# Converting all weights inside the first batch: other instructions, another place, and keys loaded first

## The chip, the cores and the metric

The kernel runs on one core of one Trainium2 chip, as one program that is launched once. The metric is the device time of an execution in microseconds (us). Engines go by the names that the profile gives them: PE (TensorE matmul), PEld (its weight loads), DVE (VectorE), ACT (ScalarE), POOL (GpSimd), SP (SyncE, which issues all transfers here).

## The reference

```python
def _attn_ref(q, k, v):                      # q, k, v: (8, 8, 576, 64) float32
    scores = scale * np.matmul(q, k.transpose(0, 1, 3, 2))
    kth = np.partition(scores, -top_k, axis=-1)[..., -top_k:-top_k + 1]      # top_k = 32
    scores = np.where(scores >= kth, scores, -1000000000.0)
    attn = np.exp(scores - np.max(scores, axis=-1, keepdims=True))
    attn = attn / (np.sum(attn, axis=-1, keepdims=True) + 1e-09)
    return np.matmul(attn, v)

def _moe_ref(x, w_theta, w_tok_r, w_tok_i, w_ch):     # x: (8, 576, 512), heads side by side
    theta = x @ w_theta
    zr, zi = x * np.cos(theta), x * np.sin(theta)
    y = np.einsum('ts,bsd->btd', w_tok_r, zr) + np.einsum('ts,bsd->btd', w_tok_i, zi)
    u = x + y
    return u + np.maximum(u @ w_ch, 0.0)
```

`reference` runs the attention and gives its output to the mixer `_moe_ref`. The four weight matrices (512x512, 576x576, 576x576, 512x512) arrive as 64-bit floats; the kernel sees each number as two 32-bit integers, a low and a high word, and makes 32-bit floats of them on the chip.

## The kernel before, in words

**Units.** The attention of a batch is done for pairs of heads, four pairs a batch. A pair's 576 queries are five units: four of 128 queries for both heads, and one (`j == NJ`) that holds the last 64 queries of both. So a batch has 20 units, and the kernel has 160. `pipeline` (line 613) walks over them. For unit `i` it emits the search for the 32nd largest score on DVE (`threshold`, `pick`, `fold`: lines 258 to 297, some 25 DVE instructions), the scores of unit `i + 2` (`scores`, line 226: matmuls into `ps_score`, then ACT's copy at line 243), the penalty and the exponential of unit `i - 1` (lines 299 to 315, ACT and POOL), transposes and the product with `v` of unit `i - 2` (lines 317 to 363), and one step of whatever stands in the list `running` (`advance`, line 638).

**Mixer.** When the last unit of a batch is through, `mixer` joins `running`. It turns the attention output, multiplies by `w_theta` (`pth`, lines 467 to 477), takes sine and cosine into the tile `z` (tag "z", a buffer of its own), multiplies by both `w_tok` (`py`, line 576) and by `w_ch` (`po`, line 601). Its matmuls run beside the units of the next batch. Behind the last unit the last mixer runs alone.

**Weights.** `widen_steps` (line 110) is the first entry of `running`: 18 jobs, four for `w_theta` (512 columns), ten for the two `w_tok` (576 columns, the remaining 64 rows of each a job of 64 partitions), four for `w_ch` (512). A job fetches 128 rows (line 129) into a buffer with tag "e", the tag of the score tiles, and converts them: ACT makes integers of the low word (line 139); DVE shifts and masks the high word (140), joins the sign bit to it (141); ACT takes its absolute value (144); POOL adds both (145); DVE sets to zero what was too small (146); for `w_theta` ACT multiplies by a constant (150). Three jobs (`WEARLY`) run ahead of the first unit, 12 steps (`WSTART`) are then let pass, and one job per unit follows. They end inside the second batch, beside the first mixer.

**The first pair.** `split_pair` (line 174) splits queries and keys into a high part (rounded, `kh`, and half of the tile `q2`) and the rest (`kl`, the other half). For the first pair SP loads all of `qT`, then all of `kT`; ACT rounds whole tiles (line 185), DVE subtracts (186).

**What sets the order.** The code gives the instructions in the order above with priorities; the tile framework's scheduler then writes one fixed order per engine, and each engine keeps to it. PSUM has three pairs of buffers: "s" for scores, "t" for transposes, "m" for `px`, `pth`, `py` and `po`.

Of the kernel before, what the change touches and what calls it, by code (L numbers as in the profile page):

```python
# [9 lines left out]
F32 = mybir.dt.float32  # L10
F32R = mybir.dt.float32r
BF16 = mybir.dt.bfloat16
I32 = mybir.dt.int32
U32 = mybir.dt.uint32
AF = mybir.ActivationFunctionType
ALU = mybir.AluOpType
AX = mybir.AxisListType

P = 128
EBUFS = 9  # L20
NQP = 1
WSTART = 12
WEARLY = 3
AHEAD = 2
S_LATE = 0
PLAN = (2, 2, 2, 2, 2)
# [8 lines left out]
STEEP = float(2.0**60)  # L35
LOWEST = -3.0e38
MAGIC = 12582912.0
SMALLEST = 1.125 * 2.0**-15
TWO_PI = 6.283185005187988
INV_TWO_PI = 0.15915494309189535  # L40
HALF_PI = 1.5707963267948966
# [3 lines left out]
def topk_attention_phase_mixer(  # L45
# [11 lines left out]
    nc = tc.nc  # L57
    B, NPAIR, _, S = qT.shape
    DM = w_ch.shape[0]
    D = P // 2  # L60
    H = 2 * NPAIR
    HS = S // 2
    NJ = S // P
    REM = S - NJ * P
    NB = DM // P
    KB = 2 * NJ + 1
# [7 lines left out]
    wk2 = ctx.enter_context(tc.tile_pool(name="wk2", bufs=2))  # L74
    wk3 = ctx.enter_context(tc.tile_pool(name="wk3", bufs=3))
    one = ctx.enter_context(tc.tile_pool(name="one", bufs=1))
    ps_s = ctx.enter_context(tc.tile_pool(name="ps_s", bufs=2, space=bass.MemoryType.PSUM))
    ps_t = ctx.enter_context(tc.tile_pool(name="ps_t", bufs=2, space=bass.MemoryType.PSUM))
    ps_m = ctx.enter_context(tc.tile_pool(name="ps_m", bufs=2, space=bass.MemoryType.PSUM))
# [22 lines left out]

    wts = {}

    def weight_tile(dtype):
        return wk2.tile([P, S], dtype, tag="w", name="w", bufs=2 * NB + KB + 1)

    def widen_steps():  # L110
        for key, n, width in (("ch", NB, DM), ("th", NB, DM), ("tok", KB, S)):
            wts[key] = [weight_tile(F32)[:, :width] for _ in range(n)]
        jobs = []
        for c in range(NB):
            jobs.append((wts["th"][c], w_theta[c * P : c * P + P], slice(0, P), INV_TWO_PI))
        for i, w in enumerate((w_tok_r, w_tok_i)):
            for c in range(NJ):
                jobs.append((wts["tok"][i * NJ + c], w[c * P : c * P + P], slice(0, P), None))
            rows = slice(i * D, i * D + D)
            jobs.append((wts["tok"][2 * NJ][rows], w[NJ * P :], rows, None))  # L120
        for c in range(NB):
            jobs.append((wts["ch"][c], w_ch[c * P : c * P + P], slice(0, P), None))
        held = {}

        def fetch(i):
            dst, src, rows, _ = jobs[i]
            n = dst.shape[-1]
            raw = wk2.tile([P, S, 2], I32, tag="e", name="wraw", bufs=EBUFS)
            nc.sync.dma_start(raw[rows, :n], src.bitcast(I32).rearrange("p (n t) -> p n t", t=2))
            held[i] = raw  # L130

        def convert(i):
            dst, _, rows, factor = jobs[i]
            n = dst.shape[-1]
            raw = held.pop(i)
            tmp = wk2.tile([P, 2, S], I32, tag="e", name="wtmp", bufs=EBUFS)
            word, tail = raw[rows, :n, 1], raw[rows, :n, 0]
            bits, low = tmp[rows, 0, :n], tmp[rows, 1, :n]
            nc.scalar.activation(low, tail.bitcast(U32), AF.Copy, scale=2.0**-29)
            nc.vector.tensor_scalar(bits, word, 3, 0x3FFFFFF8, op0=ALU.logical_shift_left, op1=ALU.bitwise_and)  # L140
            nc.vector.scalar_tensor_tensor(
                bits, word, -0x40000000, bits, op0=ALU.bitwise_and, op1=ALU.bitwise_or
            )
            nc.scalar.activation(word.bitcast(F32), word.bitcast(F32), AF.Abs)
            nc.gpsimd.tensor_add(low, low, bits)
            nc.vector.scalar_tensor_tensor(
                dst, word.bitcast(F32), SMALLEST, low.bitcast(F32), op0=ALU.is_ge, op1=ALU.mult
            )
            if factor is not None:
                nc.scalar.mul(dst, dst, factor)  # L150

        fetch(0)
        for i in range(len(jobs)):
            if i + 1 < len(jobs):
                fetch(i + 1)
            convert(i)
            yield
            if i + 1 == WEARLY:
                for _ in range(WSTART):
                    yield  # L160

    def later(n):
        return tc.high_priority(offset=-n)
# [10 lines left out]
    def split_pair(bq, p, raw):  # L174
        q2 = wk2.tile([P, 2, S], F32R, tag="q2", name="q2")
        kh = wk2.tile([P, 2, S], F32R, tag="kh", name="kh")
        kl = wk2.tile([P, 2, S], F32R, tag="kl", name="kl")
        if raw is None:

            twice = [wk2.tile([P, 2, S], F32, tag="e", name="twice", bufs=EBUFS) for _ in range(2)]  # L180
            for t, src in zip(twice, (qT, kT)):
                for a in range(2):
                    nc.sync.dma_start(t[a * D : a * D + D], src[bq, p].rearrange("(a d) s -> d a s", a=2))
            for t, hi, lo, rows in ((twice[0], q2, q2, slice(D, P)), (twice[1], kh, kl, slice(0, P))):
                nc.scalar.copy(hi, t)
                nc.vector.tensor_sub(lo[rows], t[rows], hi[rows].bitcast(F32))
        else:
            hi = wk2.tile([P, 2, S], F32R, tag="e", name="hi", bufs=EBUFS)
            nc.scalar.copy(hi, raw)
            nc.gpsimd.tensor_sub(raw.bitcast(F32R), raw, hi.bitcast(F32))  # L190
            st = {n: (hi[:, i].bitcast(F32), raw[:, i]) for i, n in enumerate("qk")}
            for a in range(2):
                sl = slice(a * D, a * D + D)
                for dst, rows, src in (
                    (q2, slice(0, D), st["q"][0]),
                    (kh, slice(0, D), st["k"][0]),
                    (kh, slice(D, P), st["k"][0]),
                    (q2, slice(D, P), st["q"][1]),
                    (kl, slice(0, D), st["k"][1]),
                    (kl, slice(D, P), st["k"][1]),  # L200
                ):
                    nc.sync.dma_start(dst[rows, a].bitcast(F32), src[sl])  # L202
        vt = wk2.tile([P, NJ, P], F32, tag="vt", name="vt")
        vr = vrem[p % 2]
        vsrc = v[bq, :, p * P : p * P + P]
        nc.sync.dma_start(vt, vsrc[: NJ * P].rearrange("(c p) d -> p c d", p=P))
        for a in range(2):
            sl = slice(a * D, a * D + D)
            nc.sync.dma_start(vr[sl, sl], vsrc[NJ * P :, sl])
        return dict(p=p, q2=q2, kh=kh, kl=kl, vt=vt, vr=vr)  # L210
# [402 lines left out]
    def pipeline():  # L613
        NU = NJ + 1
        wsteps = widen_steps()
        total = B * NPAIR * NU
        units, pairs, batches, running = {}, {}, {}, [[wsteps, []]]
# [16 lines left out]
        def split(g):  # L634
            if g < B * NPAIR:
                pairs[g] = split_pair(*divmod(g, NPAIR), pairs.get(g))
# [8 lines left out]
                            break  # L645

        split(0)
        for _ in range(WEARLY):
            next(wsteps)
        for i in range(AHEAD):  # L650
            scores(unit(i))
            fold(unit(i))
# [56 lines left out]
    def plain_batch(bq):  # L709
        bt = new_batch(bq)  # L710
        for p in range(NPAIR):
            pair = split_pair(bq, p, load_pair(bq, p))
            prev = None
            for j in range(NJ + 1):
                u = Unit(bq, bt, p, j, pair, 0, True)
                scores(u)
                fold(u)
                for _ in threshold(u):
                    pass
                penalize(u)  # L720
                exponent(u)
                turn(u, prev)
                mix_values(u)
                keep_values(u)
                prev = u
        for _ in mixer(bt):
            pass

    pipeline()

    redo = nc.values_load(flag, min_val=0, max_val=1)
    with tc.If(redo != 0):
        for _ in widen_steps():
            pass
        with tc.For_i(0, B, 1) as bi:
            plain_batch(bi)
# [38 lines left out]
```

## Time and profile before

| | us |
|---|---|
| median of 3 runs | 1308.04 (1305.59 to 1308.83) |
| the profiled execution, its own time | 1313.39 |
| its span, first to last instruction | 1311.5 |
| busy: PE / DVE / ACT / POOL | 1169.6 / 1181.1 / 1011.9 / 650.6 |

The profiled execution is one execution of its own, 5.35 us above the median of the runs, and 1.9 us of its time lie outside the span. A busy time is that of the engine's instructions, and neighbouring instructions of one engine can overlap by some hundredths of a microsecond. The end of a unit's search is marked by DVE's line 293; the last unit of the first batch has it at 166.9 us, that of the second at 323.4, that of the third at 478.0, and so on to 1216 us for the last; the 95 us behind it are the last mixer.

### The profile page before, as it was taken

The page shows a single profiled execution, that of the slowest core. Times are in us where ns is not written, and L with a number is a line of the kernel's source. Part 1 is how long each engine was busy: PE and PEld are TensorE (multiplying, and loading weights), DVE is VectorE, ACT ScalarE, POOL GpSimd, SP SyncE. Part 2 cuts the span into 40 slices and gives each one's busy share as a digit, 9 for nine tenths or more (in the row PEclk, how much of TensorE's full clock was granted, in tenths as well). Part 3 has the DMA queues.
Part 4 walks back from the last instruction along what each step waited for, and adds up shares of the span by engine and source line. Part 5 has one row for each costly group of instructions (what it writes and reads, how often), then busy time and mean ns, then how long its engine had stood idle before and what let it go on. Part 6 is the DMA issues. An engine that isn't in the chain of part 4 may idle for free.

```text
span 1311.5 us, 21746 instructions
## 1 busy us (share of the span) xinstructions
PE 1169.6 (89%) x6293; PEld 859.9 (66%) x6293; DVE 1181.1 (90%) x3993; ACT 1011.9 (77%) x2072; POOL 650.6 (50%) x768
## 2 busy tenths in 40 slices
PE   3666669899989998899999998899999999899998
PEld 3544445678657775577656785577756786567688
DVE  7999999899999999979999999889999999888453
ACT  4878778978788788977879878886888878786660
POOL 2445655744475445643465534553464544653640
PEclk9878769999989999999999999999998999999999
DMA  5234441433323333123323243123423144120001
GB/s 171 58 84 117 141 125 48 108 82 101 100 63 82 82 110 91 41 76 92 109 55 90 79 113 91 36 59 89 136 55 90 37 115 130 27 64 10 37 2 39
DMA packets 70720, 106.04 MB, mean 81 GB/s; under 512 B 13888, under 2 KB 32064, under 8 KB 70592
## 3 DMA queue, kind: packets, MB, share of 16 engines
q1 hardware_dynamic: 70592, 104.57, 29.5%
q8 instruction: 52, 0.85, 0.3%
q14 instruction: 76, 0.62, 0.2%
HBM read 38.40 MB, written 9.44 MB: 36 GB/s over the span
## 4 chain that ended last, share of the span: by engine, by line
PE 38%; DVE 32%; ACT 15%; issue 4%; POOL 4%; SPq 3%; DMA 3%; ACTq 0%; POOLq 0%; DVEq 0%
PE py L576 14%; DVE lst L283 9%; DVE lst L289 8%; PE pth L472 6%; PE px L357 5%; PE ps_score L234 4%; PE pt L329 3%; DVE lst L265 3%; DVE lo L266 3%; DVE lst L270 3%; SPq L202 3%; ACT e L314 3%; ACT pen L302 2%; PE po L601 2%; ACT e L243 2%
## 5 line engine op out<-in xcount | busy, mean ns | idle before, releaser
L304 POOL TENSOR_TENSOR e<-e,pen 128x576 f32<-128x576 f32 x288 | 369.1, 1299 | 208.4 <-ACT pen L302 195.4
L283 DVE MAX8 lst<-lst 128x8 f32<-128x192 f32 (+3 forms) x1152 | 423.9, 407 | 0.8
L289 DVE MATCH_REPLACE8 lst<-lst 128x192 f32<-128x192 f32 (+2 forms) x864 | 329.7, 388 | 0.0
L576 PE MATMUL py<-w,z 128*128 128x288 f32 x1008 | 272.0, 414 | 1.2 <-DMA z<-whole 1.2
L314 ACT ACTIVATE e<-e,lim 128x576 f32<-128x576 f32 x288 | 225.3, 784 | 36.4 <-POOL e L304 35.1
L234 PE MATMUL ps_score<-kh,q 128*128 128x288 f32 x512 | 188.9, 383 | 59.0 <-DVE lo L266 25.3
L302 ACT ACTIVATE pen<-e,lim 128x576 bf16<-128x576 f32 x288 | 210.7, 775 | 39.5 <-POOL lim L294 39.4
L576 PEld LDWEIGHTS py<-w,z 128*128 128x128 f32 x1008 | 185.7, 193 | 54.4 <-issue 7.1
L329 PE MATMUL pt<-ident,e 128*128 128x128 f32 x1152 | 178.6, 288 | 34.8 <-ACT e L314 21.1
L329 PEld LDWEIGHTS pt<-ident,e 128*128 128x128 f32 x1152 | 141.0, 146 | 76.4 <-ACT e L314 27.2
L357 PE MATMUL px<-at,vt 128*64 128x320 f32 (+1 forms) x1024 | 171.0, 430 | 7.7 <-ACT at L334 5.3
L243 ACT COPY e<-ps_score 128x576 f32<-128x576 f32 x256 | 162.0, 647 | 18.9 <-PE ps_score L234 14.7
L331 ACT COPY at<-pt 128x512 f32<-128x512 f32 x256 | 145.2, 587 | 28.0 <-PE pt L329 27.3
L234 PE MATMUL ps_score<-kl,q 128*128 128x288 f32 x512 | 157.5, 323 | 4.5 <-DMA kl<-raw 3.9
L234 PEld LDWEIGHTS ps_score<-kh,q 128*128 128x128 f32 x512 | 104.7, 205 | 81.9 <-ACT e L243 23.1
L265 DVE TENSOR_TENSOR lst<-ps_score,e 128x576 f32<-128x576 f32 (+1 forms) x160 | 109.6, 685 | 46.0 <-ACT e L243 20.9
L357 PEld LDWEIGHTS px<-at,vt 128*64 128x64 f32 x1024 | 78.4, 142 | 70.2 <-issue 19.5
L601 PE MATMUL po<-xt,w 128*128 128x288 f32 x448 | 119.4, 407 | 0.0
L270 DVE MAX8 lst<-lo 128x8 f32<-128x288 f32 x288 | 116.8, 441 | 0.0
L234 PEld LDWEIGHTS ps_score<-kl,q 128*128 128x128 f32 x512 | 105.8, 207 | 11.6 <-DMA kl<-raw 4.2
L472 PE MATMUL pth<-w,xt 128*128 128x512 f32 x224 | 107.4, 626 | 5.0 <-ACT xt L450 5.0
L266 DVE TENSOR_TENSOR lo<-ps_score,e 128x576 f32<-128x576 f32 (+1 forms) x160 | 109.6, 685 | 0.0
(119 smaller groups left out, 1676.5 us busy)
## 6 DMA issues: line engine op xcount, KB each, us to landing
kh<-hi SPq DMA_DIRECT2D x124, 144.0 KB, 2.7
kl<-raw SPq DMA_DIRECT2D x124, 144.0 KB, 2.6
raw<-in_qT_dram SPq DMA_DIRECT2D x31, 288.0 KB, 3.0
raw<-in_kT_dram SPq DMA_DIRECT2D x31, 288.0 KB, 3.1
q<-hi SPq DMA_DIRECT2D x62, 144.0 KB, 2.5
q<-raw SPq DMA_DIRECT2D x62, 144.0 KB, 2.6
vt<-in_v_dram SPq DMA_DIRECT2D x32, 256.0 KB, 2.9
out_dram<-ot SPq DMA_DIRECT2D x28, 288.0 KB, 2.2
```

The costliest lines, as they stand in the source:

```text
L234: nc.tensor.matmul(out[:, at : at + n], l, r, start=(i == 0), stop=(i == len(mm) - 1), skip_group_check=True)
L243: nc.scalar.copy(u.x[:, :, keys], u.ps[:, :, :HS])
L270: nc.vector.max(u.lst[:, w, HS:TOP], u.lo1[:, w])
L283: nc.vector.max(lst[:, w, best], part[w])
L289: nc.vector.match_replace(out=rest, in_to_replace=lst[:, w, best], in_values=part[w], imm_value=LOWEST)
L302: nc.scalar.activation(pen[:, w], u.x[:, w], AF.Relu, bias=u.lim[:, w, 0:1], scale=-STEEP)
L304: nc.gpsimd.tensor_sub(u.x[:, w], u.x[:, w], pen[:, w])
L314: nc.scalar.activation(u.x[:, w], u.x[:, w], AF.Exp, bias=u.lim[:, w, 1:2], scale=SCALE, accum_out=acc)
L329: nc.tensor.transpose(pt[:, c], e[:, w, at0 : at0 + P], ident)
L357: nc.tensor.matmul(px[sl, :n], pr["vt"][:, kb, sl], pr["at"][:, a, kb], start=(kb == 0), stop=False, skip_group_check=True)
L472: nc.tensor.matmul(th[j][: l.shape[-1]], l, r, **pos)
L576: nc.tensor.matmul(py[:, :HS], l, r, start=(i == 0), stop=(i == len(mm) - 1))
```

## The change

All 17 jobs (the two 64-row remainders are one job now) start two steps after the first unit and go on one per unit, so that they end inside the first batch. The raw words and the intermediate values lie in the first mixer's `z` buffer (`room`, two raw buffers and two intermediate ones) in place of "e" buffers. The arithmetic is another: ACT writes the scaled absolute value of the high word into a PSUM tile `size` with tag "m" (in two halves where the job has 576 columns), DVE takes the maximum with a constant there and shifts it into `room`, ACT takes the sign, POOL adds the low word and multiplies by the sign. The first pair is loaded keys first, queries in two pieces, and rounded and subtracted in pieces.

```diff
-WSTART = 12
-WEARLY = 3
+WSTART = 2
@@ widen_steps
-            rows = slice(i * D, i * D + D)
-            jobs.append((wts["tok"][2 * NJ][rows], w[NJ * P :], rows, None))
+        jobs.append((wts["tok"][2 * NJ], [w[NJ * P :] for w in toks], None))
...
+        room = one.tile([P, KB * DM], I32, tag="z", name="room")
+        raws = [room[:, i * 2 * S : (i + 1) * 2 * S].rearrange("p (n t) -> p n t", t=2) for i in range(2)]
+        tmps = [room[:, (i + 2) * 2 * S : (i + 3) * 2 * S].rearrange("p (t n) -> p t n", t=2) for i in range(2)]
...
             nc.scalar.activation(low, tail.bitcast(U32), AF.Copy, scale=2.0**-29)
-            nc.vector.tensor_scalar(bits, word, 3, 0x3FFFFFF8, op0=ALU.logical_shift_left, op1=ALU.bitwise_and)
-            nc.vector.scalar_tensor_tensor(
-                bits, word, -0x40000000, bits, op0=ALU.bitwise_and, op1=ALU.bitwise_or
-            )
-            nc.scalar.activation(word.bitcast(F32), word.bitcast(F32), AF.Abs)
+            m = n if n <= DM else n // 2
+            for c in range(0, n, m):
+                size = ps_m.tile([P, 512], F32, tag="m", name="size")[:, :m]
+                nc.scalar.activation(size, sign[:, c : c + m], AF.Abs, scale=2.0**16)
+                nc.vector.tensor_scalar(size, size, SMALLEST, None, op0=ALU.max)
+                nc.vector.tensor_scalar(bits[:, c : c + m], size.bitcast(I32), 3, None, op0=ALU.logical_shift_left)
+            nc.scalar.activation(sign, sign, AF.Sign)
             nc.gpsimd.tensor_add(low, low, bits)
-            nc.vector.scalar_tensor_tensor(
-                dst, word.bitcast(F32), SMALLEST, low.bitcast(F32), op0=ALU.is_ge, op1=ALU.mult
-            )
+            nc.gpsimd.tensor_mul(dst, low.bitcast(F32), sign)
@@ split_pair, first pair
-            for t, src in zip(twice, (qT, kT)):
+            for t, src, cols in ((tk, kT, slice(0, S)), (tq, qT, q0), (tq, qT, q1)):
...
-            for t, hi, lo, rows in ((twice[0], q2, q2, slice(D, P)), (twice[1], kh, kl, slice(0, P))):
-                nc.scalar.copy(hi, t)
-                nc.vector.tensor_sub(lo[rows], t[rows], hi[rows].bitcast(F32))
+            for w in range(2):
+                nc.scalar.copy(kh[:, w], tk[:, w])
+                nc.vector.tensor_sub(kl[:, w], tk[:, w], kh[:, w].bitcast(F32))
+            for cols in (q0, q1):
+                nc.scalar.copy(q2[:, :, cols], tq[:, :, cols])
+                nc.vector.tensor_sub(q2[D:, :, cols], tq[D:, :, cols], q2[D:, :, cols].bitcast(F32))
@@ pipeline
-        for _ in range(WEARLY):
-            next(wsteps)
```

Here `q0` is the first 128 query columns and `q1` the other 448. The constant of the maximum is 2.25.

How the instructions move, in three places. ACT at the program's start; before, conversions (lines 139 to 150) stand ahead of the first copy of scores (line 243):

```order
L185 CAST q_100<-twice 128x1152
L185 CAST kh<-twice 128x1152
L215 COPY qpad_95<-q_100 128x64 x2
L139 ACTIVATE wtmp<-wraw 128x512
L144 ACTIVATE wraw<-wraw 128x512
L139 ACTIVATE wtmp<-wraw 128x512
L144 ACTIVATE wraw<-wraw 128x512
L150 ACTIVATE w<-w 128x512
L139 ACTIVATE wtmp<-wraw 128x512
L243 COPY e<-ps_score 128x2x288 x2
```

and of the change (its line 252 is line 243 of before, and its 143, 147 and 150 are a job's three steps on ACT):

```order
L191 CAST kh<-twice 128x576 x2
L194 CAST q_100<-twice 128x2x128
L194 CAST q_100<-twice 128x2x448
L252 COPY e<-ps_score 128x2x288
L224 COPY qpad_95<-q_100 128x64 x2
L252 COPY e<-ps_score 128x2x288
L143 ACTIVATE room<-room 128x512
L147 ACTIVATE size<-room 128x512
L252 COPY e<-ps_score 128x2x288
```

The two casts become four, and the first copy of scores now follows them at once. DVE in the second batch, where the first mixer's angles are taken (line 487 before, 496 in the change); before:

```order
L487 SCALAR_TENSOR_TENSOR z<-whole,pth 128x512
L289 MATCH_REPLACE lst<-lst 128x277 x2
L283 MAX lst<-lst 128x8 x2
L146 SCALAR_TENSOR_TENSOR w<-wraw,wtmp 128x512
L283 MAX lst<-lst 128x8 x2
L289 MATCH_REPLACE lst<-lst 128x240 x2
L140 TENSOR_SCALAR wtmp<-wraw 128x512
```

and of the change:

```order
L496 SCALAR_TENSOR_TENSOR z<-whole,pth 128x512
L292 MAX lst<-lst 128x8
L298 MATCH_REPLACE lst<-lst 128x192 x2
L443 TENSOR_TENSOR xs<-px_s,rinv 64x256 x2
L292 MAX lst<-lst 128x8 x2
L302 TENSOR_REDUCE lst<-lst 128x2
L292 MAX lst<-lst 128x8 x2
```

No conversion is left beside the first mixer. ACT in the first batch, some 12 units in; before, one job's two steps (139, 144) among the work of two units:

```order
L139 ACTIVATE wtmp<-wraw 128x512
L314 ACTIVATE e,sums<-e,lim 128x576
L302 ACTIVATE pen<-e,lim 128x576 x2
L144 ACTIVATE wraw<-wraw 128x512
L369 COPY xt<-px 128x320
L331 COPY at_978<-pt 128x4x128
```

and of the change, some eight units in:

```order
L147 ACTIVATE size<-room 128x288
L143 ACTIVATE room<-room 128x576
L323 ACTIVATE e,sums<-e,lim 128x576
L311 ACTIVATE pen<-e,lim 128x576
L340 COPY at_832<-pt 128x4x128
L147 ACTIVATE size<-room 128x288
L252 COPY e<-ps_score 128x2x288
L150 ACTIVATE room<-room 128x576
```

A job has four steps on ACT here where it had two. The number of activation table loads is the same in both orders.

## Rows read from the trace of the kernel before

**Rows 1.** The page, first part: busy time, share of the span, instructions.
```profile
PE 1169.6 (89%) x6293; PEld 859.9 (66%) x6293; DVE 1181.1 (90%) x3993; ACT 1011.9 (77%) x2072; POOL 650.6 (50%) x768
```
**Rows 2.** Stretches, batches 1 to 4 and 6: length; PE, PEld, DVE, ACT, POOL busy; PEclk, DMA.
```profile
17.75:166.90 149.15, 95.38 (x468) 73.36 (x466) 147.86 (x500) 114.09 (x232) 75.94 (x86) 0.81 0.36 97
166.90:323.40 156.50, 139.01 (x707) 99.40 (x708) 151.53 (x493) 126.79 (x256) 88.67 (x98) 0.90 0.34 92
323.40:478.00 154.60, 146.64 (x802) 108.57 (x801) 150.42 (x534) 128.94 (x265) 80.31 (x98) 0.97 0.32 85
478.00:625.00 147.00, 137.93 (x749) 99.75 (x748) 135.23 (x476) 117.28 (x244) 72.30 (x91) 0.99 0.31 81
...
771.50:925.60 154.10, 145.52 (x791) 105.18 (x790) 139.83 (x487) 120.32 (x251) 74.72 (x91) 0.99 0.30 80
```
**Rows 3.** Timeline of the first 18 us: start, length, engine, line, operation, idle before.
```profile
2.19 1.26 SPq L183 DMA_DIRECT2D twice<-in_kT_dram  x2
...
6.31 1.15 ACT L185 CAST q<-twice 128x1152 fp32r<-128x1152 f32 x1 [4.07 <-DMA twice<-in_qT_dram]
...
8.98 1.15 ACT L185 CAST kh<-twice 128x1152 fp32r<-128x1152 f32 x1 [1.52 <-DMA twice<-in_kT_dram]
...
10.18 0.85 PE L234 MATMUL ps_score<-kh,q 128*128 128x288 f32 x2 [10.18 <-ACT kh L185]
...
12.94 0.44 PE L234 MATMUL ps_score<-kl,q 128*128 128x288 f32 x1
...
16.34 1.15 ACT L243 COPY e<-ps_score 128x576 f32<-128x576 f32 x2
...
17.75 0.75 DVE L265 TENSOR_TENSOR lst<-ps_score,e 128x576 f32<-128x576 f32 x1
```
**Rows 4.** DVE busy in the first two batches, lines 140, 141, 146 in turn.
```profile
17.75:166.90 149.15, 3.09 (x7) 0.81 0.36 97
166.90:323.40 156.50, 4.52 (x8) 0.90 0.34 92
17.75:166.90 149.15, 6.18 (x8) 0.81 0.36 97
166.90:323.40 156.50, 8.14 (x8) 0.90 0.34 92
17.75:166.90 149.15, 7.70 (x8) 0.81 0.36 97
166.90:323.40 156.50, 6.90 (x9) 0.90 0.34 92
```
**Rows 5.** DVE groups by form, 0 to 240 us: busy, mean ns.
```profile
L434 DVE TENSOR_TENSOR xs<-px_s,rinv 128x512 f32<-128x512 f32 x4 | 2.7, 675 | 0.0
L266 DVE TENSOR_TENSOR lo<-ps_score,e 128x288 f32<-128x288 f32 x6 | 2.7, 446 | 0.0
```
**Rows 6.** DVE timeline near 151 us, two neighbours.
```profile
150.86 0.44 DVE L265 TENSOR_TENSOR lst<-ps_score,e 128x288 f32<-128x288 f32 x1
151.22 0.44 DVE L266 TENSOR_TENSOR lo<-ps_score,e 128x288 f32<-128x288 f32 x1
```
**Rows 7.** Line 140 alone: ns min/median/max, first and last start us.
```profile
L140 DVE TENSOR_SCALAR wtmp<-wraw x18: 420/440/1492, 11.4 to 231.5; 128x512 int32<-128x512 int32 x8, 128x576 int32<-128x576 int32 x8, 64x576 int32<-64x576 int32 x2
```
**Rows 8.** ACT and POOL groups by form, 0 to 240 us.
```profile
L144 ACT ACTIVATE wraw<-wraw 128x576 f32<-128x576 f32 x8 | 6.0, 746 | 4.1 <-DVE wtmp L141 4.1
L144 ACT ACTIVATE wraw<-wraw 128x512 f32<-128x512 f32 x8 | 5.5, 681 | 2.7 <-DVE wtmp L141 2.7
L334 ACT COPY at<-pt 128x256 f32<-128x256 f32 x10 | 3.2, 378 | 1.7 <-PE pt L329 1.7
L145 POOL TENSOR_TENSOR wtmp<-wtmp 128x576 int32<-128x576 int32 x8 | 11.2, 1410 | 4.8 <-DVE wtmp L141 2.5 <-PE pt L329 2.2
```
**Rows 9.** Stretches of 12 us, columns as in rows 2.
```profile
42.00:54.00 12.00, 8.86 (x52) 6.79 (x52) 12.00 (x47) 11.39 (x25) 5.77 (x9) 0.86 0.17 51
246.00:258.00 12.00, 10.74 (x58) 7.42 (x57) 10.03 (x35) 11.20 (x25) 6.69 (x11) 1.00 0.46 124
```

More of the change, by code (lines that the diff above doesn't have):

```diff
@@ L37 @@
 MAGIC = 12582912.0
-SMALLEST = 1.125 * 2.0**-15
+SMALLEST = 1.125 * 2.0
 TWO_PI = 6.283185005187988
@@ L114, in widen_steps @@
         for c in range(NB):
-            jobs.append((wts["th"][c], w_theta[c * P : c * P + P], slice(0, P), INV_TWO_PI))
-        for i, w in enumerate((w_tok_r, w_tok_i)):
+            jobs.append((wts["th"][c], (w_theta[c * P : c * P + P],), INV_TWO_PI))
+        toks = (w_tok_r, w_tok_i)
+        for i, w in enumerate(toks):
             for c in range(NJ):
-                jobs.append((wts["tok"][i * NJ + c], w[c * P : c * P + P], slice(0, P), None))
-            rows = slice(i * D, i * D + D)
-            jobs.append((wts["tok"][2 * NJ][rows], w[NJ * P :], rows, None))
+                jobs.append((wts["tok"][i * NJ + c], (w[c * P : c * P + P],), None))
@@ L121, in widen_steps @@
+        jobs.append((wts["tok"][2 * NJ], [w[NJ * P :] for w in toks], None))
         for c in range(NB):
-            jobs.append((wts["ch"][c], w_ch[c * P : c * P + P], slice(0, P), None))
-        held = {}
+            jobs.append((wts["ch"][c], (w_ch[c * P : c * P + P],), None))
+        room = one.tile([P, KB * DM], I32, tag="z", name="room")
+        raws = [room[:, i * 2 * S : (i + 1) * 2 * S].rearrange("p (n t) -> p n t", t=2) for i in range(2)]
+        tmps = [room[:, (i + 2) * 2 * S : (i + 3) * 2 * S].rearrange("p (t n) -> p t n", t=2) for i in range(2)]
@@ L125, in fetch @@
         def fetch(i):
-            dst, src, rows, _ = jobs[i]
-            n = dst.shape[-1]
[L128 to L138, printed above, removed]
-            nc.scalar.activation(low, tail.bitcast(U32), AF.Copy, scale=2.0**-29)
-            nc.vector.tensor_scalar(bits, word, 3, 0x3FFFFFF8, op0=ALU.logical_shift_left, op1=ALU.bitwise_and)
-            nc.vector.scalar_tensor_tensor(
-                bits, word, -0x40000000, bits, op0=ALU.bitwise_and, op1=ALU.bitwise_or
-            )
-            nc.scalar.activation(word.bitcast(F32), word.bitcast(F32), AF.Abs)
+            dst, srcs, _ = jobs[i]
@@ new lines, in fetch, with convert @@
+            n = P // len(srcs)
+            for k, src in enumerate(srcs):
+                nc.sync.dma_start(
+                    raws[i % 2][k * n : k * n + n, : dst.shape[-1]],
+                    src.bitcast(I32).rearrange("p (n t) -> p n t", t=2),
+                )
+        def convert(i):
+            dst, _, factor = jobs[i]
+            n = dst.shape[-1]
+            word, tail = raws[i % 2][:, :n, 1], raws[i % 2][:, :n, 0]
+            bits, low = tmps[i % 2][:, 0, :n], tmps[i % 2][:, 1, :n]
+            sign = word.bitcast(F32)
+            nc.scalar.activation(low, tail.bitcast(U32), AF.Copy, scale=2.0**-29)
+            m = n if n <= DM else n // 2
[5 more added lines that the diff above has]
+            nc.scalar.activation(sign, sign, AF.Sign)
@@ L152, in widen_steps @@
         fetch(0)
+        for _ in range(WSTART):
+            yield
         for i in range(len(jobs)):
@@ L157, in widen_steps @@
             yield
-            if i + 1 == WEARLY:
-                for _ in range(WSTART):
-                    yield
     def later(n):
@@ L178, in split_pair @@
         if raw is None:
-            twice = [wk2.tile([P, 2, S], F32, tag="e", name="twice", bufs=EBUFS) for _ in range(2)]
-            for t, src in zip(twice, (qT, kT)):
+            tq, tk = [wk2.tile([P, 2, S], F32, tag="e", name="twice", bufs=EBUFS) for _ in range(2)]
+            q0, q1 = slice(0, P), slice(P, S)
+            for t, src, cols in ((tk, kT, slice(0, S)), (tq, qT, q0), (tq, qT, q1)):
                 for a in range(2):
-                    nc.sync.dma_start(t[a * D : a * D + D], src[bq, p].rearrange("(a d) s -> d a s", a=2))
-            for t, hi, lo, rows in ((twice[0], q2, q2, slice(D, P)), (twice[1], kh, kl, slice(0, P))):
-                nc.scalar.copy(hi, t)
-                nc.vector.tensor_sub(lo[rows], t[rows], hi[rows].bitcast(F32))
+                    nc.sync.dma_start(
+                        t[a * D : a * D + D, :, cols], src[bq, p, :, cols].rearrange("(a d) s -> d a s", a=2)
+                    )
+            for w in range(2):
[4 more added lines that the diff above has]
+                nc.vector.tensor_sub(q2[D:, :, cols], tq[D:, :, cols], q2[D:, :, cols].bitcast(F32))
         else:
```

## The prediction

> **What bounds the kernel now.** I read the page's busy times first. DVE with 90% and PE with 89% share the kernel [rows 1], so the question is which of them ends last where. The stretches by batch answer it [rows 2]. In the first batch, from the first search on, DVE is busy for 147.86 of 149.15 us and PE for only 95.38: no mixer runs yet, and DVE alone sets the pace. In the second batch DVE has 151.53 of 156.50 and PE 139.01. From the third on PE is the fuller engine, with 93.8 to 94.9% in the three later rows shown; DVE is down to 135 to 140 us in the fourth and sixth. So a microsecond taken from DVE is worth a microsecond in the first batch, part of one in the second, and little behind it. The start is a third place: the timeline shows DVE's first search at 17.75 us [rows 3], and everything later hangs on it.
>
> **The start.** Before, `q` is loaded first and rounded at 6.31; `kT` is issued from 2.19, rounded at 8.98; the first scores start at 10.18 and the last of the first unit's are begun at 12.94. Yet ACT copies them only at 16.34, because in its fixed order conversions stand ahead of that copy [rows 3]. With the change keys take the first place in SP's queue, so I let them land where queries did, at 6.3. ACT rounds two halves of about 0.6 (half of 1.15) to 7.5; the first 128 query columns are 2/9 of a tensor that took 2.7 us to follow the other (6.31 to 8.98), so they are there by 7.0; their cast ends near 7.9. DVE subtracts in pieces behind that, to about 8.8. Eight matmuls then need the 2.3 us that the old ones need without their gap, so scores end near 11.1, the first copy has been made meanwhile, and the search starts at 11.3: **minus 6.5 us**. Bounds: minus 7 if a cast hides better, minus 5 if the query piece lands with the whole tensor, at 9.0. Three early conversions lay in this gap on DVE; they cost nothing there before and now have to be paid in the first batch, below. What is queued behind `q`, `vt` and the first weights, is not needed before 11 us.
>
> **DVE in the first batch.** What goes: lines 140, 141 and 146 took 3.09, 6.18 and 7.70 us there, 17.0 in 23 instructions [rows 4]. Neighbours overlap by 0.08: the one at 150.86 is 0.44 long, and the next starts after 0.36 [rows 6]. So 23 x 0.08 = 1.9 goes off: 15.1 us are freed. What comes: all 17 jobs, two passes over PSUM each: 8 jobs of 512 columns are 16 instructions, 9 of 576 are 36 of 288 columns. The trace has no `tensor_scalar` on PSUM. Its DVE reads of PSUM take 675 ns for 512 columns and 446 for 288 [rows 5], that is 0.59 and 0.36 in the queue; in SBUF line 140 takes 420 at the least and 440 in the median, over widths of 512 and 576 [rows 7]. I take the PSUM rows, which share the memory with the new instruction: 16 x 0.59 + 36 x 0.36 = 22.4 us. **Net plus 7.3 us.** By the SBUF row, 0.34 for 512 and an estimated 0.20 for 288, it would be 12.6 us, net minus 2.5. The other bound is that the write to PSUM and the pass behind it, which reads what the first wrote, cost a third more: 30 us, net plus 15.
>
> The rows show two speeds, a median of 440 ns for 512 and 576 columns in SBUF and 446 for 288 in PSUM [rows 5, 7]. The Trainium skill (VectorE: DVE Perf Modes, "Why PSUM operands drop a tier") says that a 32-bit operand in PSUM loses the mode with two read ports that a `tensor_scalar` in SBUF has. By that rule the sum stays at plus 7.3, and without it would be at minus 2.5; no run here shows it for this instruction yet.
>
> **The second batch.** The three lines had 4.52 + 8.14 + 6.90 = 19.6 us there in 25 instructions [rows 4], 17.6 in the queue, and all of it goes. DVE then needs about 134 of the 156.5 us, and PE's 139 set the end. The fourth batch, with 137.93 of PE and 135.23 of DVE, takes 147.0 [rows 2]; I let the second do the same: **minus 9.5 us**. Bounds: minus 2.2, if it takes the 154.3 (mean) of the third and sixth, and minus 17.6, all of DVE's part. From there on the batches hold the same work as before; the orders differ in detail, which I price at plus or minus 4 us.
>
> **ACT in the first batch.** A job has two steps of about 0.71 on ACT before [rows 8], 8 jobs there 11.4 with a multiplication of 0.7. The change has three of 0.68 for 512 columns, and for 576 two of 0.746 and two of 288 columns, estimated 0.40 from the 256-column row [rows 8]: 8 x 2.04 + 9 x 2.29 + four multiplications of 0.68 = 39.6, less 4 for overlaps of neighbours. So ACT goes from 114.09 to some 138 us of 149.15 + 7.3 = 156.5: 88%. Does DVE wait then? At 11.39 of 12 us on ACT, DVE ran on without a gap; at 11.20 of 12, in another stretch, it had 10.03 [rows 9]. I estimate that two thirds of the batch would be that full: the bounds are zero and 105/12 x 2.0 = 17 us. I take the low end, **plus 2 us**, because scores are made two units ahead and ACT has slack in the stretches between.
>
> **POOL, PSUM, SP.** POOL gets 34 instructions of at most 1.41 and loses 8 [rows 8], so 75.94 goes to about 112 us of 156: nothing, while ACT's and DVE's work covers it; without that cover an exponential waits up to 2.8 us for a job in front of its subtraction. `size` shares the pair "m" with `px`: the product with `v` can wait for a shift on DVE, and PE has 54 us of idle time in this batch to hide that. A fetch on SP waits for POOL's multiplication two jobs back, and copies of the next pair stand behind it; they have two units. The buffer "z" is free when the first mixer's angles come, units after the last job.
>
> **Sum**: -6.5 + 7.3 - 9.5 + 2.0 = -6.7 us. The profiled execution took 1313.39, so it would be 1306.7; against the median of the runs, 5.35 lower, **1301.3 us**.
>
> **Rivals.**
> *A. The second batch does not get shorter.* It takes 154.3, as the third and sixth do, the sixth with 139.83 of DVE [rows 2], little more than the 134 that it will have. For it: PE at 95% there, and the order holds the first mixer's last products back until the third batch. Against: the fourth. -6.5 + 7.3 - 2.2 + 2.0 = +0.6: 1308.6.
> *B. ACT becomes the bound of the first batch* (slower). ACT keeps an order too; if its waits for POOL, PE and transfers stay what they are, its idle time of 149.15 - 114.09 = 35 us comes on top of 138: 173 in place of 156.5, plus 16.5 instead of 2: +7.8, 1315.8. It decides from 18.5 us of idle time on, and the kernel is slower from some 30. For it: the full stretch with DVE at 10.03. Against: the idle time is there because DVE sets the pace, so it should shrink.
> *C. DVE's passes in PSUM run at SBUF's pace.* -2.5 in place of +7.3: 1291.5, less if ACT then bounds. Against it: rows 5; for it, nothing but line 140.
> *D. The change doesn't do what it says*: a sign function could bring table loads on ACT. Both orders have equally many, so I leave it 2%.
>
> **How the numbers follow.** Forecast 50%, with its own range 1296 to 1307; A 22%; B 18%; C 8%; D 2%. A measurement of this kernel can tell some 0.3% from no change, here 3.9 us: faster is below 1304.1, slower above 1312.0. The forecast gives 38 points to faster and 12 to no change; C gives 8 to faster; A, with the spread of 4, 7 to faster, 11 to no change, 4 to slower; B 14 to slower, 4 to no change; D 2 to no change: 0.53, 0.29, 0.18. The range must hold A and the middle of B, and leave out C's end: 1293 to 1315.
>
> **What would show it.** In the profile after: the first search at 11 to 12 us; the maximum and the shift with 0.67 us for 512 columns and 0.45 for 288, none stretched; the first batch's end near 167 as before, the second's near 314; ACT at 85 to 90% of the first batch with DVE above 97%. Wrong would be: DVE waiting for ACT's copies or for `size` in the first batch (B), a second batch of 154 us with PE at 95% (A), or half-length passes (C). It would be wrong altogether if later batches, whose work is the same, differed by more than 4 us in sum.

## The result: 1.1% faster, and the profile after

| | before | after |
|---|---|---|
| median of 6 runs, us | 1309.09 (1305.59 to 1313.34) | 1295.1 (1290.59 to 1298.9) |
| ratio to before, 95% interval | | 0.9891 (0.9863 to 0.9919) |
| the profiled execution, us | 1313.39 | 1298.9 |

The change takes 14.0 us off, clear of what the measurement can't tell from no change. The forecast was 1301.3; the time lies in the range, but the gain is twice the 6.7 us of the sum. A second measurement of the unaltered change, in another session, gave 0.9894 (0.9873 to 0.9915).

The stretches of the profile after, first batch to fourth, columns as in [rows 2]; the batches end here by the last search of a batch (line 302 on DVE, line 293 before):

```profile
11.00:167.44 156.44, 103.10 (x469) 73.53 (x467) 155.00 (x529) 134.20 (x277) 101.93 (x109) 0.72 0.44 128
167.44:300.30 132.86, 119.80 (x624) 85.08 (x625) 128.28 (x458) 112.49 (x233) 76.08 (x92) 0.95 0.30 76
300.30:454.50 154.20, 148.10 (x805) 107.35 (x805) 142.54 (x496) 122.29 (x254) 75.06 (x93) 0.99 0.30 79
454.50:598.40 143.90, 137.37 (x740) 99.14 (x737) 136.66 (x481) 119.73 (x248) 76.98 (x93) 0.98 0.32 85
```

The first batch ends at 167.44 us, as before (166.9): it begins earlier and is longer. DVE is busy for 155.00 of its 156.44 us, so ACT, with 134.20, can have cost it 1.4 us at the most. The second batch looks 24 us shorter than the 156.50 of [rows 2], but searches and mixer are shifted against each other in the new order, and the third, with 154.20, is longer than the third before. For that one [rows 2] has a wrong mark, and with it for the fourth and the sixth. The last unit of a batch holds 64 queries of both heads in one list of 128, so its row of line 293 writes 128x1. The row behind 478.0 writes 128x2: it is the first unit of the fourth batch.

```profile
464.52 0.14 DVE L293 TENSOR_REDUCE lst<-lst 128x1 f32<-128x4 f32 x1
477.93 0.15 DVE L293 TENSOR_REDUCE lst<-lst 128x2 f32<-128x8 f32 x1
```

The third, fourth and sixth batches before, at their true ends, columns as in [rows 2]:

```profile
323.40:464.50 141.10, 133.14 (x718) 97.83 (x717) 136.92 (x485) 118.83 (x245) 74.85 (x93) 0.96 0.31 82
464.50:615.60 151.10, 142.03 (x777) 102.64 (x778) 139.33 (x490) 119.68 (x248) 73.91 (x91) 0.99 0.31 81
758.80:916.10 157.30, 148.72 (x808) 107.09 (x808) 142.55 (x496) 120.67 (x252) 72.47 (x90) 0.99 0.29 78
```

A fairer mark than the end of a search is the end of a mixer. DVE's last row of the first and of the second mixer (start, length, line, operation), before:

```profile
338.13 0.44 DVE L602 SCALAR_TENSOR_TENSOR ot<-po,xt 128x288 f32<-128x288 f32 x1
...
492.36 0.43 DVE L602 SCALAR_TENSOR_TENSOR ot<-po,xt 128x288 f32<-128x288 f32 x1
```

and after:

```profile
331.80 0.43 DVE L611 SCALAR_TENSOR_TENSOR ot<-po,xt 128x288 f32<-128x288 f32 x1
...
480.18 0.43 DVE L611 SCALAR_TENSOR_TENSOR ot<-po,xt 128x288 f32<-128x288 f32 x1
```

By these marks the span's 14.4 us come as +0.5 up to the first batch's end (167.44 for 166.9), -12.7 from there to the second mixer's end (480.18 - 167.44 = 312.7 for 325.5), and -2.2 behind it (to 1297.1 and 1311.5).

Of the 12.7 us, 6.9 come up to the first mixer's end (331.80 - 167.44 = 164.4 for 171.2) and 5.8 between both ends (148.4 for 154.2). Where the first part arises is seen in the 36 us behind the first batch. Two stretches of 18 us before, columns as in [rows 2]:

```profile
168.00:186.00 18.00, 12.13 (x53) 7.81 (x53) 18.00 (x52) 12.25 (x26) 12.10 (x10) 0.69 0.42 125
186.00:204.00 18.00, 14.46 (x54) 9.10 (x56) 17.81 (x52) 14.33 (x28) 10.41 (x11) 0.66 0.56 159
```

and after:

```profile
168.00:186.00 18.00, 14.17 (x70) 9.90 (x71) 18.00 (x66) 15.12 (x34) 12.74 (x16) 0.81 0.55 145
186.00:204.00 18.00, 16.79 (x80) 9.74 (x79) 17.52 (x60) 13.84 (x30) 7.18 (x11) 1.00 0.01 5
```

DVE is full in all four, or nearly so. Before, conversions take 2.27 + 5.55 + 2.94 = 10.8 us of its 36 there (lines 140, 141, 146); after, two last ones end within the first eight. PE does 150 matmuls in place of 107, at a granted clock of 0.81 and 1.00 in place of 0.69 and 0.66. The clock matters for what a busy microsecond is worth: from one matmul to the next, scores of 288 columns take 0.24 us where these traces have a granted clock of 0.50 and 0.13 where they have 1.00, transposes 0.21 and 0.11, `py` 0.48 and 0.24. Counted with the steps at 1.00 (0.13 us for scores and, on average, for `px`, 0.11 for a transpose, 0.24 for `py` and `po`, 0.43 for `pth`), PE has done 61 us of work by 168 us in both kernels, and 77 before and 85 after by 204. So PE's 26.6 busy microseconds of these 36 before held only 16 us of work. The lead of 8 us lasts, at 194 and 201 us of work by 336 us, as PE is full from about 250 us to the first mixer's end in both.

The second part arises behind it, where no conversion runs in either kernel. From the first mixer's end to the second's, before and after:

```profile
338.13:492.36 154.23, 145.50 (x790) 107.21 (x786) 150.25 (x533) 127.66 (x266) 78.11 (x97) 0.97 0.33 86
331.80:480.18 148.38, 142.18 (x771) 102.95 (x769) 136.72 (x477) 119.22 (x246) 74.29 (x89) 0.99 0.31 82
```

By the first mixer's end, 41 units' searches were through before and 43 after; by the second's, 62 in both. Before, DVE still catches up two units there and is busy for 150.25 of 154.23 us. That this backlog is what costs the 5.8 us fits the rows; no experiment isolates it.

The start, rows of the timeline as in [rows 3]:

```profile
6.32 1.24 ACT L191 CAST kh<-twice 128x576 fp32r<-128x576 f32 x2 [4.07 <-DMA twice<-in_kT_dram]
...
8.96 0.61 PE L243 MATMUL ps_score<-kh,q 128*128 128x288 f32 x1 [8.96 <-DVE q L195]
...
10.32 0.64 ACT L252 COPY e<-ps_score 128x576 f32<-128x576 f32 x1 [0.72 <-PE ps_score L243]
...
11.28 0.64 ACT L252 COPY e<-ps_score 128x576 f32<-128x576 f32 x1
...
11.96 0.76 DVE L274 TENSOR_TENSOR lst<-ps_score,e 128x576 f32<-128x576 f32 x1 [1.23 <-ACT e L252]
```

The search starts at 11.96 us in place of 17.75. The new DVE passes, groups by form from 0 to 240 us (busy, mean ns, idle before):

```profile
L148 DVE TENSOR_SCALAR size<-size 128x288 f32<-128x288 f32 x18 | 8.1, 456 | 0.0
L149 DVE TENSOR_SCALAR room<-size 128x288 int32<-128x288 int32 x18 | 7.9, 444 | 0.0
L148 DVE TENSOR_SCALAR size<-size 128x512 f32<-128x512 f32 x8 | 5.5, 687 | 0.1
L149 DVE TENSOR_SCALAR room<-size 128x512 int32<-128x512 int32 x8 | 5.4, 675 | 0.0
```

They take what reads of PSUM took before [rows 5], and 26.9 us in all, against 42 for lines 140, 141 and 146. One job, with a pass of each line, still falls behind the first batch's end.

### The profile page after: what moved, and what is told of

Read it like the earlier page. It is cut to its first block, busy times and chain, and to the rows that moved or that the text cites. A ratio compares the mean times of both kernels' runs of the same rounds, so it can differ in the third digit from the quotient of the medians.

```text
span 1297.1 us, 21711 instructions
## 1 busy us (share of the span) xinstructions
PE 1168.7 (90%) x6293; PEld 852.4 (66%) x6293; DVE 1165.8 (90%) x3993; ACT 1018.5 (79%) x2098; POOL 663.1 (51%) x784
## 4 chain that ended last, share of the span: by engine, by line
DVE 32%; PE 32%; ACT 22%; POOL 4%; SPq 3%; issue 3%; DMA 3%; ACTq 0%; DVEq 0%; POOLq 0%
PE py L585 11%; DVE lst L292 10%; DVE lst L298 9%; PE pth L481 6%; PE px L366 4%; ACT e L323 4%; ACT pen L311 4%; DVE lst L274 3%; DVE lo L275 3%; DVE lst L279 3%; ACT e L252 3%; PE ps_score L243 3%; SPq L211 3%; ACT at L340 3%; PE pt L338 2%
## 5 line engine op out<-in xcount | busy, mean ns | idle before, releaser
L313 POOL TENSOR_TENSOR e<-e,pen 128x576 f32<-128x576 f32 x288 | 365.3, 1286 | 195.2 <-ACT pen L311 184.3
L292 DVE MAX8 lst<-lst 128x8 f32<-128x296 f32 (+3 forms) x1152 | 424.1, 406 | 0.9
L298 DVE MATCH_REPLACE8 lst<-lst 128x277 f32<-128x277 f32 (+2 forms) x864 | 329.2, 386 | 0.0
L243 PE MATMUL ps_score<-kh,q 128*128 128x288 f32 x512 | 186.3, 378 | 56.4 <-DVE lo L275 30.9
L366 PE MATMUL px<-at,vt 128*64 128x320 f32 (+1 forms) x1024 | 174.9, 440 | 4.5 <-ACT at L343 4.5
```

The lines of the kernel that those rows point to most:

```text
L243: nc.tensor.matmul(out[:, at : at + n], l, r, start=(i == 0), stop=(i == len(mm) - 1), skip_group_check=True)
L292: nc.vector.max(lst[:, w, best], part[w])
L298: nc.vector.match_replace(out=rest, in_to_replace=lst[:, w, best], in_values=part[w], imm_value=LOWEST)
L313: nc.gpsimd.tensor_sub(u.x[:, w], u.x[:, w], pen[:, w])
L366: nc.tensor.matmul(px[sl, :n], pr["vt"][:, kb, sl], pr["at"][:, a, kb], start=(kb == 0), stop=False, skip_group_check=True)
```

## The experiments

The theory: DVE sets the pace of the first batch, PE that of what follows as soon as DVE doesn't hold it up any more; the change gains because it takes conversions from DVE behind the first batch and makes them cheap enough for the first. Each experiment moves one part. Every run stands against before in its own session. Each edit lets the scheduler write another order of the whole program, so a difference of a few us has two sources; the last experiment measures that.

### Keys first alone

```diff
+ before.py, with the new loading and splitting of the first pair; WEARLY = 3, WSTART = 12 stay
```

> The kernel before with only the new loading of the first pair (keys first, in pieces). Theory (DVE sets the pace of the first batch, and its start is set by ACT's fixed order): three conversions still stand ahead of the first copy of scores, so the first search starts only about 1 us earlier than 17.75, and the time is 1306 to 1310 where before has 1309. Rival (the gain of the change is the earlier loading): the first search near 12 us and 1303 or less.

Measured: 1307.13 us, ratio 1.0001 (0.9982 to 1.0019). The search starts at 17.08. ACT's timeline shows why:

```profile
15.10 0.65 ACT L139 ACTIVATE wtmp<-wraw 128x512 int32<-128x512 uint32 x1
15.66 1.15 ACT L249 COPY e<-ps_score 128x576 f32<-128x576 f32 x2
```

The copies of scores wait behind the third job's first step, as before. The earlier keys alone gain nothing.

### The new place with the old arithmetic

```diff
-WSTART = 12
-WEARLY = 3
+WSTART = 2
+ fetch(0), then WSTART steps let pass, then a job per unit; keys first; lines 139 to 146 and the "e" buffers stay
```

> Keys first and all jobs from the second step on, one per unit, but with the old arithmetic (three DVE instructions a job) and the old buffers. Theory: first search near 12 us, first batch longer than the change's by some 18 jobs x 2.1 us less 26 us of the change = 10 to 15 us, so its last search ends near 180 us; the second batch gains as in the change: 1303 to 1309. Rival (only the place counts, DVE's passes do not): 1295 as in the change.

Measured: 1310.52 us, ratio 1.0015 (0.9997 to 1.0033), a little past the theory's 1309 and far from the rival. The search starts at 11.65, but the first batch ends at 183.07 only, 15.6 us behind the change. One stretch from 12 us to that end, and the old passes by form:

```profile
12.00:183.00 171.00, 106.27 (x471) 79.11 (x470) 170.25 (x537) 130.13 (x255) 94.29 (x96) 0.75 0.41 117
```

```profile
L140 DVE SCALAR_TENSOR_TENSOR wtmp<-wraw,wtmp 128x576 int32<-128x576 int32 x8 | 7.6, 952 | 0.0
...
L139 DVE TENSOR_SCALAR wtmp<-wraw 128x512 int32<-128x512 int32 x8 | 6.6, 819 | 0.0
```

DVE is full (170.25 of 171). Its old passes cost 40 us there, where those of the change cost 26.9. The one in SBUF that takes 420 ns at best [rows 7] has a mean of 819 in the eight passes of 512 columns; the eight of 576 columns have 483. The long mean comes of two passes, of 1185 and 2428 ns, that ran beside an instruction of POOL:

```profile
149.94 2.63 POOL L194 TENSOR_TENSOR raw<-raw,hi 128x1152 fp32r<-128x1152 f32 x1 [0.63 <-ACT hi L193]
150.42 2.43 DVE L139 TENSOR_SCALAR wtmp<-wraw 128x512 int32<-128x512 int32 x1
```

The Trainium skill (SBUF — State Buffer, "Who interferes with whom") says that DVE and GpSimd share a pair of ports as a lock, which such a pass and one with two SBUF inputs need, and an instruction outside the two-port modes with one SBUF input at most does not. The runs agree: of the change's 26 maxima, many beside a busy POOL, none took more than 700 ns.

```profile
L148 DVE TENSOR_SCALAR size<-size x26: 445/460/700, 13.8 to 168.2; 128x288 f32<-128x288 f32 x18, 128x512 f32<-128x512 f32 x8
```

### The new arithmetic in the old place

```diff
+ before.py's place (WEARLY = 3, WSTART = 12) and "e" buffers, keys first
+ line 139, then Abs into size (PSUM), max and shift on DVE, Sign on ACT, add and multiply on POOL
```

> Keys first and the new arithmetic (PSUM, sign by GpSimd), but the old buffers and the old place (three jobs ahead, the others one per unit from the twelfth unit on). Theory: DVE is relieved by some 4 us in the first batch and 6 to 8 in the second, of which PE takes a part: 1300 to 1304. Rival (place counts, arithmetic does not): 1307 to 1311.

Measured: 1320.34 us, ratio 1.0087 (1.0058 to 1.0117): slower than before, against both expectations. The first batch ends at 153.76, 13 us earlier. The second mixer ends late:

```profile
504.92 0.45 DVE L609 SCALAR_TENSOR_TENSOR ot<-po,xt 128x288 f32<-128x288 f32 x1
```

that is 12.6 us behind 492.36. The stretch in which conversions run beside the first mixer, before and here:

```profile
204.00:252.00 48.00, 41.02 (x194) 25.64 (x194) 45.97 (x142) 43.04 (x86) 33.84 (x38) 0.93 0.29 76
204.00:252.00 48.00, 40.63 (x184) 25.21 (x183) 37.09 (x120) 45.42 (x92) 37.61 (x40) 0.96 0.32 85
```

ACT is busy for 45.42 of 48 us, and DVE for 37.09 in place of 45.97. Each job brings ACT one more step or two here, where the mixer's copies, sines and absolute values already load it.

### The same with less on ACT

```diff
-            nc.scalar.activation(low, tail.bitcast(U32), AF.Copy, scale=2.0**-29)
-            nc.scalar.activation(sign, sign, AF.Sign)
-            nc.gpsimd.tensor_add(low, low, bits)
-            nc.gpsimd.tensor_mul(dst, low.bitcast(F32), sign)
+            nc.gpsimd.tensor_mul(low.bitcast(F32), bits.bitcast(F32), bits.bitcast(F32))
+            nc.gpsimd.tensor_mul(dst, low.bitcast(F32), bits.bitcast(F32))
```

> The new arithmetic in the old place and the old buffers, as in the third experiment (1320 us), without ACT's steps for the low word and the sign (the weights come out as a third power of a truncated magnitude; POOL's two steps stay). Theory (beside the first mixer ACT is full, and two more steps a job there cost DVE and PE their pace): 1306 to 1313. Rival (an unlucky order alone made the third experiment slow, ACT's load did not): 1317 to 1323.

Measured: 1305.32 us, ratio 0.9977 (0.9958 to 0.9997), 15 us less than with the two steps on ACT. The second mixer ends in time:

```profile
491.15 0.43 DVE L607 SCALAR_TENSOR_TENSOR ot<-po,xt 128x288 f32<-128x288 f32 x1
```

```profile
204.00:252.00 48.00, 39.67 (x189) 25.08 (x187) 32.98 (x103) 38.82 (x78) 33.29 (x35) 0.93 0.31 85
```

So the two steps on ACT did make the third experiment slow, by far more than the few us that another order is worth (last experiment). But the way there is not the one that I had read from its stretch: DVE is no busier now (32.98 us). Part of the time comes back ahead of that stretch, as the first `pth` starts at 197.3 us here and at 203.9 in the third experiment, and part of it behind. Which wait carries it stays open.

### The change with the old loading

```diff
+ after.py, with before's loading and splitting of the first pair
```

> The change with the old loading of the first pair, queries first and whole. Theory: the first search comes some 2 to 4 us later than 11.96, as one conversion slips ahead of the copy of scores again, and the whole kernel with it: 1297 to 1299 where the change has 1295. Rival (a later start is caught up, as the first batch is not bound by it): 1295.

Measured: 1300.04 us, ratio 0.9938 (0.9916 to 0.996), some 5 us more than the change, and a little past the theory's 1299. The first search:

```profile
13.82 0.76 DVE L268 TENSOR_TENSOR lst<-ps_score,e 128x576 f32<-128x576 f32 x1 [0.58 <-ACT e L246]
```

1.9 us later than in the change, and one job's steps are ahead of ACT's first copy again. The loading that gains nothing alone is worth some of the 14 us here, 2 by the start and the rest within what an order is worth.

### One more step on ACT per job

```diff
             nc.scalar.activation(sign, sign, AF.Sign)
+            nc.scalar.activation(sign, sign, AF.Sign)
```

> The change with the sign taken twice: one more ACT step of 0.6 to 0.7 us in each of the 17 jobs, some 10.5 us more on ACT in the first batch, 145 in place of 134 of 156 us. Theory (DVE alone is the bound there, ACT's idle time shrinks to make room): no more than 3 us longer, 1295 to 1298. Rival (ACT is as good as full): 6 to 10 us longer, 1301 to 1305, with DVE waiting for ACT's copies in the first batch.

Measured: 1299.08 us, ratio 0.9924 (0.991 to 0.9938), between both. The two halves of the first batch, columns as in [rows 2]:

```profile
12.00:84.00 72.00, 42.08 (x189) 31.97 (x189) 72.00 (x248) 59.22 (x118) 39.62 (x45) 0.67 0.41 111
84.00:156.00 72.00, 45.08 (x229) 31.27 (x228) 71.50 (x249) 69.80 (x148) 54.02 (x56) 0.74 0.49 139
```

In the second, ACT is busy for 69.80 of 72 us, and DVE still for 71.50; the batch ends at 164.97. The rival's sign, DVE waiting for ACT in the first batch, is not there. So the 4 us are not lost in the first batch; where they are, this profile can't tell, as its execution (1307.62) is the slowest of its runs.

### The maximum twice, and not at all

```diff
                 nc.vector.tensor_scalar(size, size, SMALLEST, None, op0=ALU.max)
+                nc.vector.tensor_scalar(size, size, SMALLEST, None, op0=ALU.max)
```

> The change with the maximum in PSUM taken twice: 26 more DVE instructions of 0.687 and 0.456 us, 11.4 us in the queue. Theory (DVE is the bound of the first batch and what is added there is passed on to the end): 9 to 12 us longer, 1304 to 1307. Rival (the pace is set elsewhere): under 3 us longer.

Measured: 1313.59 us, ratio 1.0039 (1.0024 to 1.0054), 18 us more than the change and slower than before.

```profile
175.60 0.15 DVE L303 TENSOR_REDUCE lst<-lst 128x1 f32<-128x4 f32 x1
```

The first batch ends 8.2 us later than in the change, and the loss has more than doubled by the second mixer's end. What is added to DVE in the first batch is passed on, and more; the theory had 9 to 12 us. The opposite edit takes the line out:

```diff
-                nc.vector.tensor_scalar(size, size, SMALLEST, None, op0=ALU.max)
```

> The change without the maximum on DVE, which guards the conversion of numbers below some 2^-126 in magnitude; the weights of this reference have none, other inputs could. 26 DVE instructions less, 11.4 us in the queue. Theory (DVE is the bound of the first batch): 8 to 12 us shorter, 1283 to 1287; a little less if ACT, with 134 us of then 145, comes in the way. Rival (ACT or POOL bound it as soon as DVE gets lighter): 1291 or more.

Measured: 1299.48 us, ratio 0.9927 (0.9913 to 0.994), not shorter than the change but 4 us longer. The first batch does end earlier:

```profile
160.55 0.15 DVE L301 TENSOR_REDUCE lst<-lst 128x1 f32<-128x4 f32 x1
```

6.9 us before 167.44, yet the runs don't show it at the end. In number the rival came true (1291 or more, ACT or POOL as the bound as soon as DVE gets lighter). Its first batch from 12 us on:

```profile
12.00:160.55 148.55, 94.80 (x441) 69.41 (x441) 141.12 (x497) 127.04 (x263) 99.29 (x106) 0.77 0.47 133
```

DVE is no longer full (141.12 of 148.55), and the lead is gone before the mixer begins: its first `pth` starts at 191.1 us, in the change at 191.0. So DVE was the bound, with another close behind it, and relief of DVE alone paid nothing. Which wait holds the mixer back stays open; the profiled execution (1295.64) is the fastest of its runs, that of the change (1298.9) the slowest, so the ends of both traces can't be compared.

### Score buffers in place of the room

```diff
+ after.py, with raw and tmp in tiles of tag "e" (EBUFS = 9), as before
```

> The change with its raw words and intermediate values in score buffers (tag e) as before, in place of the first mixer's room. Theory (buffers are no bound as long as DVE is busy all the time): 1294 to 1299. Rival (two of nine score buffers taken by a job hold up the loads of the next pair and the scores): 1302 or more, with DVE idle in the first batch.

Measured: 1298.99 us, ratio 0.9922 (0.9906 to 0.9939). The room is worth 4 us at the most, inside the theory's range, but not quite for its reason: DVE waited 8.3 us for ACT's copies in the first 250 us where the change had 2.8.

### No conversion

```diff
+            nc.scalar.copy(dst, word.bitcast(F32))
-            (everything else in convert but the multiplication for w_theta)
```

> The change with the conversion left out but for one copy on ACT per job (the weights come out as the high words taken as floats); no DVE and no POOL step is left, ACT loses some 20 us. Theory (DVE is the bound of the first batch, and its 22.4 us in the queue are passed on): 15 to 23 us shorter than the change, 1272 to 1280. Rival (what is saved before the first mixer is not passed on, as PE is the bound from there on): 1285 or more.

Measured: 1281.86 us, ratio 0.98 (0.9773 to 0.9828), 13.3 us under the change: short of the theory's 15 to 23, and still under the rival's 1285. The first batch ends 14.8 us earlier:

```profile
152.60 0.13 DVE L291 TENSOR_REDUCE lst<-lst 128x1 f32<-128x4 f32 x1
```

DVE was no longer full in it (133.27 of 140.6 us, by its stretch from 12 to 152.6), so of 22.4 us taken off some 7 turned into idle time, and the rest was passed on nearly in full. This is what the conversion still costs. As ACT and POOL lost their steps too, the edit doesn't tell DVE's part from theirs; the one without the maximum does.

### Another order of the same work

```diff
-WSTART = 2
+WSTART = 3
```

> The change with its jobs beginning one unit later (third step in place of the second), the same work in the same batch. It measures what another fixed order of the same instructions is worth. Theory (order is worth some 4 us either way): 1292 to 1299. Rival (the change owes most of its gain to a lucky order): 1302 or more.

Measured: 1298.35 us, ratio 0.9931 (0.9907 to 0.9956): 3 us more than the change for the same instructions one unit later. The change itself, measured once more in that session:

> The change itself once more, unaltered, beside the three others of this call and beside before. Both theories: a ratio near 0.989 to before, 1293 to 1297 us. It fixes what the earlier experiments are compared with, above all the one without the maximum (0.9927).

1295.2 us, 0.9894 (0.9873 to 0.9915). Four neighbours of the change that should be within a few us of it, or faster (one more step on ACT, score buffers, no maximum, one unit later) all came out at 1298.4 to 1299.5. So some 3 to 4 us of the 14 look like the luck of this order rather than its work. Only the last of the four is neutral, and its interval overlaps the change's a little (0.9907 to 0.9956, and 0.9873 to 0.9915). No version that computes the whole reference was faster than the change.

## Why the prediction was right, and what it sized wrong

*What bounds the kernel.* Right for the first batch, with a limit that I didn't see. DVE is full in it before and after, and the edits that add to its work (the maximum twice, the place alone) make it 15 to 18 us longer than the change. The one that only takes from it gained nothing at the end, as something else was close behind.

*The start*, minus 6.5: measured -5.8 (11.96). Keys landed at 6.32, the first scores began at 8.96 for 8.8 forecast. What I had left out is that the search waits for the second copy too (11.28 to 11.92), and that copy for PE's eighth matmul, which ended at 11.24.

*DVE in the first batch*, plus 7.3: the passes took 687, 675, 456 and 444 ns where rows gave 675 and 446. The rule on PSUM operands in the Trainium skill (VectorE: DVE Perf Modes, "Why PSUM operands drop a tier") is borne out: a `tensor_scalar` of 512 columns took 420 ns at best in SBUF [rows 7] and 675 here. Rival C, with 8%, is out.

*ACT in the first batch*, plus 2: nothing. ACT came to 134.2 us, 86%, for 88% forecast, and DVE stayed full with one more step per job on ACT. Rival B is out for this batch. In the third experiment, where conversions run beside the first mixer, ACT's steps did cost 15 us. The three terms make +2.8 at the first batch's end; it was +0.5, as DVE's and ACT's together came to +6.3 (155.5 us from the first search to the batch's end, for 149.2) in place of +9.3.

*The second batch*, minus 9.5: -12.7 to the second mixer's end. This is the term that was mis-sized, in two ways. First, I took PE's 139.01 us of [rows 2] as work that stays, and removed only idle time. But a part of these busy microseconds was PE at a granted clock of 0.66 to 0.69, and the same matmuls take less at 1.00: 26.6 of them held 16 us of work. With the conversions gone from there, PE had both, fewer gaps and a faster clock. Second, the length that I gave the batch, 147.0, came from a wrong mark. The fourth batch takes 151.1, and the third and sixth 149.2 on average: the same reasoning gives -5.4, and rival A -7.3 in place of -2.2. So the 9.5 lay nearer to the measured 12.7 by luck, and rival A's 154.3 has no batch behind it. That the second batch gets no shorter is out by the mixers' marks.

*Behind it*, nothing plus or minus 4: -2.2 in the profiled executions. Together with the first batch's 2.3 and the second's 3.2 that is the 7.7 us between the span's 14.4 and the sum; the runs' 14.0 are 7.3 over it. By the neighbours, half of that surplus is the order.

*The change doesn't do what it says* (D): no. POOL's 34 steps, some of 1.4 us, cost nothing that a row shows, with 101.93 of 156.44 us busy.

## What to carry to other kernels

Two edits that gain nothing or lose apart, 1.0015 and 1.0087 here, can gain together: the cheap arithmetic was dear by its steps on ACT where conversions run beside the mixer, and the early place was dear for DVE with the old arithmetic. Ask of each stage which engine has room, and price a move with the instructions that it will run there. When a bottleneck is taken from a stage where the clock of PE was low, price the matmuls at the full clock as well as the gaps. Tell the end of a stretch by the shape of its row and not by the line alone, before a price is read from it. Where a scheduler rewrites the whole order, measure a neutral edit before giving the last 0.3% a cause.

## What the runs showed of the hardware that was not expected

A DVE `tensor_scalar` that reads and writes PSUM took 687 ns for 512 columns, hardly more than the one that reads PSUM and writes SBUF (675). ACT's absolute value into PSUM took 639 ns for 512 columns where the one in SBUF took 681 [rows 8]. PE's granted clock in the first batch was 0.72 on average with 103.10 of 156.44 us busy, lower than before (0.81 with 95.38 of 149.15), and it cost nothing there, as DVE set the pace.
